# Angle tables grown on VectorE in 256 columns, set-up queues reordered, idle matmuls on zeros, one guard maximum and key copies shared out, in a kernel of multi-query attention beside a diagonal state-space layer

## The chip, the cores and the metric

The kernel runs on one core of a Trainium2 chip. The metric is device microseconds of one execution, lower is better. Engines: TensorE (PE, matmuls into PSUM), VectorE (DVE), ScalarE (ACT, activations), GpSimd (POOL) and SyncE (SP, which issues most DMAs; ScalarE's queue issues a few). Each engine takes its instructions in the order in which the program has them and waits on semaphores.

## What is computed

Two independent layers, whose outputs are put side by side (2048 x 1280, bf16). Layer A is a diagonal state-space layer: 640 complex states, a scan over 2048 steps, and a projection back. Layer B is attention with 32 heads of 20 columns that share one key and one value head:

```python
# A
Lam_bar = exp(dt * Lam)                       # 640 complex numbers
h[t] = Lam_bar * h[t-1] + x[t] @ B_bar.T      # 2048 steps
y = 2 * (h @ Cmat.T).real + x * Dskip
# B
q = (x @ wq).reshape(1, 2048, 32, 20)         # 32 heads
k, v = x @ wk, x @ wv                         # one head, 20 columns
o = softmax(q @ k.T * 20 ** -0.5) @ v
out = o.reshape(1, 2048, 640) @ wo
```

## The kernel before

Attention sets the course. Its scores are cut into 2048 units of 128 keys x 512 (query, head) columns: 32 groups (8 groups of 4 heads in each of 4 query blocks), each of 4 heads x 16 key blocks. A unit is filled by TensorE (QK) into a PSUM bank, turned into weights, and taken by TensorE into the PV accumulator. Most units go to ScalarE as an exponential (L1362) over a tile of three banks (R0) or two (R1), in turn; ten tiles of results (P) can be waiting for PV. The others go to VectorE, which makes the weights by integer arithmetic (L1368, then the shifts L1374). Such a unit is allowed only when the set-up work (`rest`) and the table growth (`grow`) are done. The first group is taken in two halves: group -1 has keys 0 to 1023 with a guard (a bound on the scores) from those keys alone, group 0 the other 1024 keys with the guard of all; a factor (`frac`, L649) joins them, and VectorE's L1411 carries the first half out of the accumulator.

The order on every engine is written by a planner in the program (`Plan`, `main`). It keeps a clock for each engine, prices each operation (`occ`) and takes from the candidates the one that could begin first, with a bias for each kind and some random noise; 64 seeds, one for each 64th of the units, set the biases and the noise. What it writes is fixed at build time: on the chip each engine follows that order and waits where a partner is late. The set-up up to the first exponential is written by hand in `setup`, in program order.

The set-up, by engine. SyncE issues ten transposing loads of B_x (`xbT`, blocks `0a` to `4a` of steps 0 to 1023, then `0b` to `4b`), then all of wq, then other things. ScalarE's queue issues log_dt, Lambda_im, wk, wv and the first 80 columns of wq. ScalarE pads wk to four heads (`wk4`, four copies, L521); the angle base table `tm` (128 steps, 5 blocks, sine and cosine) is made by VectorE (L753 to L756) and ScalarE (L758, L759). TensorE multiplies xbT by wk4 into B0 and B1 (512 keys each); VectorE takes the absolute maximum of each (L597) and makes the guard matrix Mblk from both (L605); ScalarE copies each twice to KT (L586); TensorE adds the guard to the queries of the first group in R0, VectorE copies them to QT (L846), and the first fill can start. `spin` matmuls (L553) between these write what nobody reads, into R0; they read wk4 and xbT.

Behind it, by the planner: the keys of the second half (`rest`: maximum over both banks L638, copies to KT by VectorE L590, the new guard `again`, 80 columns of wq, padded, as `wq1`, L651), the values (`vals`: 80 matmuls of 20 columns into PV, then four scaled copies to VP, L632), and the tables. The tables hold cos and sin for 512 steps: columns 0 to 127 are the base; each of the 30 other pieces of 128 columns is a product on GpSimd (L779, base times a rotation's sine) and a sum on VectorE (L781, base times its cosine plus or minus that product). Behind the 30 products GpSimd makes Md's mask (L690) and reorders wq to `wqd` (L656, five copies), from which later query groups are computed (`qd_block`).

## Time and profile before

| | |
|---|---|
| median of 3 runs | 762.35 us (760.70 to 762.83) |
| the profiled execution | 761.37 us |
| its span, first to last instruction | 759.5 us |
| mean granted TensorE clock | 0.988 |
| busy: TensorE, VectorE, ScalarE, GpSimd | 700.3, 716.0, 735.1, 369.4 us |
| ScalarE idle between the first and the last exponential | 11.4 us |
| first exponential starts, last one ends | 16.76, 750.82 us |

A timeline row gives the start in us, the time from the first to the last end of a run of like instructions, engine, line, operation, what it writes and reads with shapes, how many there are, and in brackets the idle time of the engine before it and who ended that. "PE R L453" as a releaser is a matmul into the score tiles. A row of windows gives a stretch, its length, the busy time of PE, weight loads, DVE, ACT and POOL with the number of instructions, the granted clock, the DMA share and GB/s.

### The profile page before, as it was taken

Reading aid. Unit: us, or ns where it says so; the run is one execution under the profiler, and the core shown is the slowest. Engines: PE = TensorE matmul, PEld = TensorE weight load, DVE = VectorE, ACT = ScalarE, POOL = GpSimd, SP = SyncE. Lnnn points to the kernel's source line nnn. Section 1 sums busy time; section 2 is a strip of 40 time slices with the busy share of each in tenths; the row PEclk is TensorE's granted clock in tenths of the full one; section 3 lists DMA queues with packets and bytes.
Section 4 is the critical chain, followed back from the end, with each engine's and each line's share of the span. In section 5 each row is a group of like instructions: output and inputs, shape, how many; then the busy total and the mean of one; then the engine's idle time right before and its main releaser. Section 6 shows DMA issues by size and latency. Waiting matters only on the chain.

```text
span 759.5 us, 22797 instructions
## 1 busy us (share of the span) xinstructions
PE 700.3 (92%) x9703; PEld 227.5 (30%) x9705; DVE 716.0 (94%) x1117; ACT 735.1 (97%) x702; POOL 369.4 (49%) x739
## 2 busy tenths in 40 slices
PE   6699997888899999999899999999999999989997
PEld 2222222222222334332222333332223333223433
DVE  5889999999998999999999899999999899999976
ACT  6769999999999999999999999999999999999996
POOL 7922235443998450009976602057982472880040
PEclk9979999999999999999999999999999999999999
DMA  9265601000002010230002011040000211000121
GB/s 178 61 109 120 129 22 45 13 23 3 16 10 66 17 43 29 57 60 15 16 10 51 25 35 40 18 93 23 3 16 22 76 33 33 18 15 9 37 54 36
DMA packets 61330, 31.89 MB, mean 42 GB/s; under 512 B 41638, under 2 KB 61230, under 8 KB 61230
## 3 DMA queue, kind: packets, MB, share of 16 engines
q1 hardware_dynamic: 59078, 30.12, 16.9%
q8 instruction: 77, 1.26, 0.7%
q10 hardware_dynamic: 2152, 0.32, 0.3%
q14 instruction: 23, 0.19, 0.1%
HBM read 9.21 MB, written 12.69 MB: 29 GB/s over the span
## 4 chain that ended last, share of the span: by engine, by line
ACT 78%; PE 12%; DVE 7%; POOL 2%; issue 1%; ACTq 0%
ACT P L1362 77%; PE B L453 5%; PE R L453 4%; PE PV L453 3%; DVE Pd L1374 2%; POOL Pd L779 2%; DVE Pd L1368 2%; DVE cs L781 1%; DVE tm L991 1%; DVE hh L1019 1%; ACTq L426 0%; DVE KT L590 0%; DVE VP L632 0%; ACT L515 0%; DVE mabs L638 0%
## 5 line engine op out<-in xcount | busy, mean ns | idle before, releaser
L1362 ACT ACTIVATE P<-R 128x1024 bf16<-128x1024 f32 (+1 forms) x677 | 722.3, 1297 | 11.4 <-PE R L453 7.2
L453 PE MATMUL R<-QT,KT 32*128 32x512 bf16 (+1 forms) x1684 | 266.2, 387 | 36.3 <-ACT P L1362 26.9
L453 PE MATMUL PV<-P,VP 128*32 128x512 bf16 x1586 | 270.7, 389 | 5.1 <-DVE VP L632 3.9
L453 PE MATMUL PV<-Pd,VP 128*32 128x512 bf16 x1848 | 269.4, 385 | 2.5 <-DVE OTr L1416 0.9
L1368 DVE TENSOR_SCALAR Pd<-B 128x512 int16<-128x512 f32 x364 | 246.1, 683 | 16.9 <-PE B L453 14.9
L1374 DVE TENSOR_SCALAR Pd<-Pd 128x1536 int16<-128x1536 int16 (+3 forms) x338 | 243.4, 727 | 2.8
L1007 POOL TENSOR_TENSOR tm<-hh,cs 128x128 bf16<-128x128 f32 x320 | 163.9, 535 | 156.9 <-DVE hh L1019 140.7
L453 PEld LDWEIGHTS R<-QT,KT 32*128 32x128 bf16 (+1 forms) x1684 | 66.4, 91 | 292.8 <-ACT P L1362 261.5
L453 PE MATMUL B<-QT,KT 32*128 32x512 bf16 x364 | 140.8, 387 | 0.0
L1007 POOL TENSOR_TENSOR W<-tm 128x128 bf16<-128x128 bf16 x160 | 81.6, 533 | 36.0 <-PE B L453 31.8
L453 PEld LDWEIGHTS PV<-Pd,VP 128*32 128x32 bf16 x1848 | 64.6, 94 | 66.4 <-issue 43.0
L453 PEld LDWEIGHTS PV<-P,VP 128*32 128x32 bf16 x1586 | 63.8, 94 | 57.9 <-issue 42.6
L1101 POOL TENSOR_TENSOR OTd<-OTd,rwide 128x128 bf16<-128x128 bf16 x80 | 33.6, 447 | 80.1 <-DMA OTd<-o_rows 78.2
L1368 DVE TENSOR_SCALAR Pd<-R 128x512 int16<-128x512 f32 x98 | 66.8, 682 | 2.3 <-PE R L453 2.0
L947 POOL TENSOR_SCALAR tm<-W,sc 128x128 f32<-128x128 bf16 x40 | 33.9, 860 | 55.8 <-DMA W<-in_A_C_im_dram 20.7
L991 DVE TENSOR_TENSOR tm<-B,cs 128x1024 bf16<-128x1024 f32 x40 | 48.5, 1214 | 0.8 <-PE B L453 0.7
L453 PE MATMUL B<-CGre,W 128*32 128x384 bf16 (+1 forms) x640 | 47.7, 303 | 0.1
L453 PE MATMUL B<-CGim,W 128*32 128x384 bf16 (+1 forms) x640 | 47.1, 299 | 0.0
L1019 DVE TENSOR_TENSOR_SCAN hh<-sc,hini,B 128x512 f32<-128x512 f32 x30 | 37.7, 1269 | 0.4 <-PE B L453 0.4
L453 PEld LDWEIGHTS B<-QT,KT 32*128 32x128 bf16 x364 | 33.0, 91 | 0.0
L453 PE MATMUL B<-xaT,BTim 128*32 128x512 bf16 x400 | 31.0, 383 | 0.0
L453 PE MATMUL B<-xbT,wqd 128*32 128x512 bf16 x400 | 30.8, 400 | 0.0
(163 smaller groups left out, 466.2 us busy)
## 6 DMA issues: line engine op xcount, KB each, us to landing
o_rows<-OTr SPq DMA_DIRECT2D x32, 128.0 KB, 1.7
QT<-q_rows SPq DMA_DIRECT2D x30, 128.0 KB, 2.3
q_rows<-Qd SPq DMA_DIRECT2D x16, 160.0 KB, 2.9
OTd<-o_rows SPq DMA_DIRECT2D x16, 160.0 KB, 3.3
out_dram<-ystage SPq DMA_DIRECT2D x16, 160.0 KB, 1.8
out_dram<-ostage SPq DMA_DIRECT2D x12, 160.0 KB, 1.8
CGre<-in_B_wq_dram SPq DMA_DIRECT2D x1, 800.0 KB, 7.2
WO<-in_B_wo_dram SPq DMA_DIRECT2D x4, 200.0 KB, 4.9
```

Source lines behind the costliest of these rows:

```text
L453: ins = e.matmul(o() if callable(o) else o, lhsT=l, rhs=r, start=st, stop=sp, skip_group_check=True, **kw)
L779: pool(lambda e, c=c, i=i, s=s, tmp=tmp: e.tensor_scalar(tmp, K.base[:, 1 - i, c, :], s, None, op0=ALU.mult), self.base_keys + ["rot"], [t ...
L781: grow.append(Op("dve", lambda e, c=c, i=i, co=co, tmp=tmp, k=k: e.scalar_tensor_tensor(out=K.cs[:, c, i, 128 * k:128 * k + 128], in0=K.ba ...
L947: pool(lambda e, y=y, c=c, gy=gy, i=i: e.tensor_scalar(K.ctmp[:, i:i + 128], y[:, i:i + 128], sc[:, gy, c:c + 1], None, op0=ALU.mult), key ...
L991: dve(lambda e, k=k, h=h: e.tensor_tensor(K.tm[:, 2 * k:2 * k + 2, :], bass.AP(tensor=K.BB, offset=512 * int(h.key[1]), ap=[[512 * self.BA ...
L1007: put(lambda e, c0=c0, end=end: e.tensor_tensor(out[:, c0:end], a[:, c0:end], b[:, c0:end], op), reads, [writes + h], n, gate=None if i el ...
L1019: dve(lambda e, ri=ri, ini=ini, h=h: e.tensor_tensor_scan(K.hh[:, ri, :], dec, h.T[:, :], ini, ALU.mult, ALU.add), ["sc", None, "hini"], [ ...
L1101: ops.append(Op("pool", lambda e, c=c, m=m: e.tensor_tensor(K.OTd[:, m, c], K.OTd[:, m, c], K.rwide[:, c], ALU.mult), rw + [f"OTe{dd}" for ...
L1362: return Op("act", lambda e: e.activation(dst, K.R[n % 2][:, 0:512 * size], ACT.Exp, scale=self.exp_scale), [f"R{n % 2}"] + ["R0c"] * (siz ...
L1368: return Op("dve", lambda e: e.tensor_scalar(K.Pd[:, 0, u, :], K.B[x][:, :], self.d_off, 0.0, op0=ALU.add, op1=ALU.max), [key], [f"Pd{u}_0 ...
L1374: return Op("dve", lambda e: e.tensor_scalar(K.Pd[:, i:i + n, a:b, :].rearrange("p s u n -> p s (u n)"), K.Pd[:, 0:n, a:b, :].rearrange("p ...
```

## The change

1. Growth of the tables: no product on GpSimd. VectorE makes 15 products of 256 columns (sine and cosine together, fp32) and 15 sums of 256 columns; a third base plane holds the negated first one (one more VectorE operation), so that both halves are a subtraction.
2. Queues: wv's load goes from ScalarE's queue to SyncE's, between the two halves of xbT. On GpSimd half_pi comes first, and the zeros in OTr's second half come right behind the identity.
3. wk4 is filled by one VectorE copy instead of four ScalarE copies.
4. Idle matmuls read the identity and those zeros, and there are 14 instead of 9: three at the very start, three after the bias rows, one among the key matmuls; the four and three behind stay.
5. One maximum over both banks (1024 columns) instead of two and a combination; the guard product is a tensor_scalar.
6. Keys 512 to 1023 are copied to KT by VectorE, behind the query copy, instead of by ScalarE. KT is tracked in blocks of 128 keys; group 0 may start when the new queries are there and a fill waits only for its own keys.
7. The planner's biases for `rest`, `vals` and `grow` differ, and all but a few of the 64 seeds. So the order of everything behind the set-up is another one. The whole order has 447 two-bank exponentials instead of 445, with 232 three-bank ones as before.

VectorE, from the end of its memsets to the first VP copies and the new query copy, before:

```order
L597 TENSOR_REDUCE mabs<-B 128x1 x2
L605 SCALAR_TENSOR_TENSOR Mblk<-mabs,Pd 128x128
L846 TENSOR_SCALAR QT<-R 128x512
L763 CAST cs<-tm 128x10x128
L781 SCALAR_TENSOR_TENSOR cs<-tm,rot,Pd 128x128 x19
L632 TENSOR_SCALAR VP<-PV 128x16x20 x4
L617 TENSOR_TENSOR mabs<-mabs 128x1
L638 TENSOR_REDUCE mabs<-B 128x1
L617 TENSOR_TENSOR mabs<-mabs 128x1 x2
L590 TENSOR_SCALAR KT<-B,half 128x512 x2
```

The same stretch now (the line numbers are those of the changed file; L789 is a product, L791 a sum):

```order
L859 TENSOR_SCALAR QT<-R 128x512
L588 TENSOR_SCALAR KT<-B,half 128x512 x2
L615 TENSOR_SCALAR tm<-tm 128x640
L772 CAST cs<-tm 128x10x128
L789 TENSOR_SCALAR Pd<-tm,rot 128x256 x2
L791 SCALAR_TENSOR_TENSOR cs<-tm,rot,Pd 128x2x128
L789 TENSOR_SCALAR Pd<-tm,rot 128x256
L791 SCALAR_TENSOR_TENSOR cs<-tm,rot,Pd 128x2x128
L789 TENSOR_SCALAR Pd<-tm,rot 128x256
L791 SCALAR_TENSOR_TENSOR cs<-tm,rot,Pd 128x2x128
L643 TENSOR_REDUCE mabs<-B 128x1
L618 TENSOR_TENSOR mabs<-mabs 128x1 x2
```

Nineteen sums stood ahead of VP; now four products and three sums stand ahead of the second maximum, and behind it come two key copies, the guard product and VP.

GpSimd, behind the constants of the mask, before:

```order
L576 TENSOR_TENSOR sc<-sc,sv 128x5
L779 TENSOR_SCALAR Pd<-tm,rot 128x128 x30
L688 MEMSET Md 128x160
L690 AFFINE_SELECT Md<-Md 128x160 x4
L656 COPY wqd<-CGre 128x640 x5
```

And now:

```order
L603 TENSOR_TENSOR sc<-sc,sv 128x5
L693 MEMSET Md 128x160
L695 AFFINE_SELECT Md<-Md 128x160 x4
L661 COPY wqd<-CGre 128x640 x5
L664 TENSOR_SCALAR nident<-ident 128x128
```

The five copies to wqd stand right behind Md's mask; they wait for the load of wq.

VectorE, ahead of the copy to wq1 (L651 before, L656 now), before:

```order
L646 TENSOR_SCALAR Mblk<-Pd,mabs 128x128
L781 SCALAR_TENSOR_TENSOR cs<-tm,rot,Pd 128x128 x3
L651 COPY wq<-CGre 128x20x20
L781 SCALAR_TENSOR_TENSOR cs<-tm,rot,Pd 128x128 x4
L842 TENSOR_SCALAR Qabs<-B 128x512
```

And the last rows ahead of it now:

```order
L789 TENSOR_SCALAR Pd<-tm,rot 128x256
L820 RECIPROCAL sc<-sc 128x5
L791 SCALAR_TENSOR_TENSOR cs<-tm,rot,Pd 128x2x128
L789 TENSOR_SCALAR Pd<-tm,rot 128x256
L791 SCALAR_TENSOR_TENSOR cs<-tm,rot,Pd 128x2x128
L656 COPY wq<-CGre 128x20x20
```

Between the mask product (L651 now) and that copy stand eight sums, seven products and the reciprocal, where three sums stood; behind it three products and four sums, the last ones around the query copies.

The core of the diff:

```diff
-    SPIN = 1, 4, 3
+    SPIN = 3, 3, 1, 4, 3
+    HEAD = 8
-    SEEDS = (111, 1209, 2445, 3180, 4815, 5028, 6775, 7124, 8575, 9354, 10399, 11278, 12878, 13810, 14176,
+    SEEDS = (172, 1183, 2925, 3286, 4369, 5158, 6349, 7538, 8807, 9403, 10689, 11086, 12883, 13390, 14424,
...
         for i, h in enumerate("ab"):
+            if i:
+                go(self.dma(K.wv_raw, t["wv"].rearrange("(c p) n -> p c n", p=128), "wv", writes=["wv_raw"], kb=25))
             for c in range(NC):
...
-        go(self.dma(K.wv_raw, t["wv"].rearrange("(c p) n -> p c n", p=128), "wv", writes=["wv_raw"], kb=25, q="act"))
...
+        def spin(n):
+
+            for i in range(n):
+                go(self.mms([self.m1(K.R[0][:, 0:512], K.ident[:, :], K.OTr[:, 1, :], True, True)], ["ident", "OTr1"], ["R0"],
+                            accum=True))
...
-        for j in range(4):
-            act(lambda e, j=j: e.activation(K.wk4[:, :, 32 * j:32 * j + 20], K.wk_raw[:, :, :], ACT.Copy),
-                ["wk_raw", "wk4"], ["wk4"], n=100)
...
-        for i in range(2):
-            dve(lambda e, i=i: e.tensor_reduce(out=mcol(i), in_=K.B[i][:, :], axis=AX.X, op=ALU.max,
-                                               apply_absolute_value=True), [f"B{i}"], [f"mabs{i}"], n=512)
+        dve(lambda e: e.tensor_reduce(out=mcol(3), in_=K.BB[:, 0:h0], axis=AX.X, op=ALU.max, apply_absolute_value=True),
+            ["B0", "B1"], ["mabs3"], n=h0)
...
-        for tb in range(2):
-            for o in copy("act", tb):
-                go(o)
...
+        for o in copy("act", 0):
+            go(o)
...
+        dve(lambda e: e.tensor_scalar(K.Mblk[:], K.mask, mcol(3), None, op0=ALU.mult), mk + ["mabs3"], ["Mblk"], n=128)
...
+        for o in copy("dve", 1):
+            go(o)
+        dve(lambda e: e.tensor_scalar(K.base[:, 2], K.base[:, 0], -1.0, None, op0=ALU.mult), self.base_keys, self.base_keys, 640, 2)
...
+        dve(lambda e: e.tensor_copy(wk4[:, :, :, 0:20], wk), ["wk_raw", "wk4"], ["wk4"], n=400)
...
-                for i in range(2):
-                    m = 2 * (3 * c + k - 1) + i
-                    tmp, tk = K.flat[:, 4608 + 128 * m:4736 + 128 * m], f"gt{m}"
...
-                    pool(lambda e, c=c, i=i, s=s, tmp=tmp: e.tensor_scalar(tmp, K.base[:, 1 - i, c, :], s, None, op0=ALU.mult),
-                         self.base_keys + ["rot"], [tk], 0.385)
...
+                prods.append(Op("dve", lambda e, c=c, s=s, tmp=tmp: e.tensor_scalar(tmp, K.base[:, 1:3, c, :], s, None, op0=ALU.mult),
+                                self.base_keys + ["rot"] + rows, [tk], occ=dve_t(256, 1.4)))
+                sums.append(Op("dve", lambda e, c=c, co=co, tmp=tmp, k=k: e.scalar_tensor_tensor(
+                    out=K.cs[:, c, :, 128 * k:128 * k + 128], in0=K.base[:, 0:2, c, :], scalar=co, in1=tmp, op0=ALU.mult,
+                    op1=ALU.subtract), self.base_keys + ["rot", tk] + rows, [f"cs{c}{i}{k}" for i in range(2)],
+                    occ=dve_t(256) + 0.06))
...
-                reads |= {f"KT{j % 2}_{kc // 4}", f"QT{g % self.QRING}"}
+                reads |= {f"KT{j % 2}_{kc}", f"QT{g % self.QRING}"}
...
-                    bias = 0.0 if own else self.wait - 0.1 * (name == self.first)
+                    bias = (0.12 if name == "vals" else -0.4 * (o is again[0]) if name == "rest" else 0.0) if own else self.wait - 0.1 * (name == self.first)
...
+                elif name == "grow":
+                    bias = 0.3 if rest or self.vals else 0.05
```

More of the change, by code (lines that the diff above doesn't have):

```diff
@@ L417, in do, with dma @@
         self.go(Op(*a, **k))
[L419 removed]
+    def dma(self, out_ap, in_ap, key, reads=(), writes=(), tr=False, kb=100, q="sp", lat=None, **k):
         nc = self.nc
@@ L601, in setup @@
               occ=act_t(512), lat=0.12))
-        for tb in range(2):
-            for o in copy("act", tb):
-                go(o)
-        dve(lambda e: e.scalar_tensor_tensor(out=K.Mblk[:], in0=wide(1), scalar=mcol(0), in1=K.mask, op0=ALU.max,
-                                             op1=ALU.mult), mk + ["mabs0", "mabs1"], ["Mblk"], n=128)
-        spin(self.SPIN[1])
+        for o in copy("act", 0):
+            go(o)
+        s, lre, NRE = self.s_ops[0], self.s_ops[3], 1
+        pool(lambda e: e.tensor_tensor(s(NRE), s(0), lre, ALU.mult), ["sc", "sv0"], ["sc"])
+        act(lambda e: e.activation(s(self.RDEC), s(NRE), ACT.Exp), ["sc"], ["sc"], n=5)
+        dve(lambda e: e.tensor_scalar(K.Mblk[:], K.mask, mcol(3), None, op0=ALU.mult), mk + ["mabs3"], ["Mblk"], n=128)
+        spin(self.SPIN[3])
         va = [self.v_part(0, c) for c in range(NC)]
@@ L620, in setup @@
         top.done = lambda: self.max_done.add(0)
-        last = list(copy("dve", 3))
-        last[-1].done = lambda: self.qt_done.add(0)
+        more, last = (list(copy("dve", i)) for i in (2, 3))
+        self.kt_ready = self.HEAD
+        for x, n in ((more, 12), (last, 16)):
+            x[-1].done = lambda n=n: setattr(self, "kt_ready", n)
         self.max_done = set()
@@ L1444, in main @@
                     out, d = pick(size, d)
+                if g in qt_done and all(left[gx][j][-1] < self.kt_ready for gx, j in out):
                     o = fill_op(n, out, d, x)
```

129 lines of the change are left out of this document (66 added, 63 removed), and 8 rows, old and new, of the table SEEDS.

## The prediction

> **What bounds the kernel now.** I read the page first (its shares, the chain that ended last, the costliest groups), then ScalarE's busy time stage by stage, then each engine's timeline of the first 50 us.
>
> ```profile
> span 759.5 us, 22797 instructions
> ...
> ACT 78%; PE 12%; DVE 7%; POOL 2%; issue 1%; ACTq 0%
> ...
> L1362 ACT ACTIVATE P<-R 128x1024 bf16<-128x1024 f32 (+1 forms) x677 | 722.3, 1297 | 11.4 <-PE R L453 7.2
> ...
> L453 PE MATMUL PV<-P,VP 128*32 128x512 bf16 x1586 | 270.7, 389 | 5.1 <-DVE VP L632 3.9
> ```
>
> The exponentials on ScalarE hold 722.3 of 759.5 us and are 78% of the chain. In the next table (stretch, its length, then each engine's busy time) the ACT column shows where they are not fed.
>
> ```profile
> 16.80:25.00 8.20, 6.54 (x90) 3.23 (x89) 6.68 (x19) 8.19 (x7) 7.83 (x13) 1.00 0.54 173
> 25.00:50.00 25.00, 18.45 (x159) 4.48 (x160) 22.69 (x40) 14.77 (x14) 16.80 (x29) 0.73 0.46 67
> 50.00:250.00 200.00, 179.97 (x2177) 51.40 (x2178) 193.52 (x296) 199.60 (x184) 104.28 (x186) 0.99 0.21 46
> 250.00:500.00 250.00, 241.62 (x3566) 80.80 (x3563) 242.47 (x373) 249.56 (x240) 100.28 (x210) 1.00 0.13 33
> 500.00:750.80 250.80, 238.72 (x3511) 79.63 (x3503) 238.80 (x363) 250.51 (x236) 127.59 (x267) 1.00 0.12 31
> 750.80:759.50 8.70, 5.49 (x174) 4.14 (x170) 3.35 (x6) 1.43 (x3) 0.00 (x0) 0.94 0.22 77
> ```
>
> From 50 to 750.8 us ScalarE idles 0.40 + 0.44 + 0.29 = 1.1 us. From 25 to 50 it idles 10.2 us. The span is therefore a sum: start of the first exponential, 722.3 us of exponentials, 10.2 + 1.1 us of waits, 0.4 us of another activation, and 8.7 us of tail. The change can reach the first and third terms. ScalarE's timeline:
>
> ```profile
> 14.34 2.41 ACT L586 ACTIVATE KT<-B,half 128x512 bf16<-128x512 f32 x4
> 16.76 8.23 ACT L1362 ACTIVATE P<-R 128x1536 bf16<-128x1536 f32 x7
> 28.18 1.02 ACT L1362 ACTIVATE P<-R 128x1024 bf16<-128x1024 f32 x1 [3.19 <-PE R L453]
> 39.85 2.36 ACT L1362 ACTIVATE P<-R 128x1536 bf16<-128x1536 f32 x2 [2.42 <-PE B L453]
> 44.95 1.02 ACT L1362 ACTIVATE P<-R 128x1024 bf16<-128x1024 f32 x1 [2.73 <-PE R L453]
> ```
>
> TensorE, in whose order these waits arise:
>
> ```profile
> 7.90 1.04 PE L453 MATMUL B<-xbT,WO 128*128 128x512 bf16 x2 [2.63 <-ACT WO L521]
> 13.31 1.03 PE L453 MATMUL R<-xbT,WO 128*128 128x512 bf16 x4
> 15.11 0.39 PE L453 MATMUL R<-Qabs,Mblk 128*128 128x512 bf16 x1 [0.58 <-ACT KT L586]
> 27.42 0.40 PE L453 MATMUL PV<-P,VP 128*32 128x512 bf16 x4 [3.92 <-DVE VP L632]
> 37.59 1.67 PE L453 MATMUL B<-xbT,wq 128*32 128x512 bf16 x20 [2.13 <-DVE wq L651]
> 42.29 0.62 PE L453 MATMUL B<-Qabs,Mblk 128*32 128x512 bf16 x4 [1.40 <-DVE Qabs L842]
> ```
>
> VectorE, which is waited for there:
>
> ```profile
> 5.72 0.85 DVE L753 TENSOR_TENSOR Pd<-hh,ang 128x640 f32<-128x640 f32 x1
> 6.60 0.49 DVE L754 TENSOR_SCALAR Pd<-Pd 128x640 f32<-128x640 f32 x1
> 13.08 1.29 DVE L597 TENSOR_REDUCE mabs<-B 128x1 f32<-128x512 f32 x2 [2.56 <-PE B L453]
> 14.48 0.48 DVE L605 SCALAR_TENSOR_TENSOR Mblk<-mabs,Pd 128x128 bf16<-128x128 f32 x1
> 17.53 4.69 DVE L781 SCALAR_TENSOR_TENSOR cs<-tm,rot,Pd 128x128 bf16<-128x128 f32 x14
> 22.73 1.51 DVE L781 SCALAR_TENSOR_TENSOR cs<-tm,rot,Pd 128x128 bf16<-128x128 f32 x3 [0.50 <-POOL Pd L779]
> 25.69 1.67 DVE L632 TENSOR_SCALAR VP<-PV 128x320 bf16<-128x320 f32 x4
> 27.41 1.21 DVE L638 TENSOR_REDUCE mabs<-B 128x1 f32<-128x1024 f32 x1
> 28.93 1.40 DVE L590 TENSOR_SCALAR KT<-B,half 128x512 bf16<-128x512 f32 x2
> 30.25 0.28 DVE L643 TENSOR_SCALAR Mblk<-Pd,mabs 128x128 bf16<-128x128 f32 x1
> 34.10 3.06 DVE L781 SCALAR_TENSOR_TENSOR cs<-tm,rot,Pd 128x128 bf16<-128x128 f32 x3
> 37.36 4.27 DVE L781 SCALAR_TENSOR_TENSOR cs<-tm,rot,Pd 128x128 bf16<-128x128 f32 x4
> ```
>
> GpSimd, on whose products the first sums wait and beside whose copies the last ones run:
>
> ```profile
> 12.55 19.69 POOL L779 TENSOR_SCALAR Pd<-tm,rot 128x128 f32<-128x128 f32 x30
> 34.34 6.76 POOL L656 COPY wqd<-CGre 128x640 bf16<-128x640 bf16 x5
> ```
>
> VectorE is held at GpSimd's pace in the middle of the 19 table sums that stand ahead of VP, so VP comes late, TensorE stands 3.92 us at its first PV matmul, and the fills behind it starve ScalarE (3.19 us). Later the sums that run beside GpSimd's five wqd copies delay wq1 and Qabs, and TensorE stands there (2.13, 1.40).
>
> **The change, part by part.** *Start.* The wv issue (0.78, below) leaves ScalarE's queue and half_pi becomes GpSimd's first constant, so the first table load, and with it the angle chain, comes about 0.8 us earlier: L753's work at 4.9 instead of 5.72. The padded key weights follow as one VectorE copy and are ready near 6.0, where ScalarE's four copies released TensorE at 7.9. Then the data decides; issues on SyncE's and ScalarE's queues, and the median time to landing:
>
> ```profile
> 0.79 13.78 SPq L424 DMA_TRANSPOSE xbT<-in_B_x_dram  x10
> 2.11 0.78 ACTq L426 DMA_DIRECT2D WO<-in_B_wv_dram  x1
> ```
>
> ```profile
> xbT<-in_B_x_dram SPq DMA_TRANSPOSE x10, 4.1
> ...
> CGre<-in_B_wq_dram SPq DMA_DIRECT2D x1, 800.0 KB, 7.2
> WO<-in_B_wv_dram ACTq DMA_DIRECT2D x1, 25.0 KB, 4.6
> ```
>
> The fifth transpose is issued at 0.79 + 4 x 1.38 = 6.3 and lands at 10.4. Behind it stand two matmuls. Warm, four take 1.03 us (the row at 13.31); cold, two take 1.04 (7.90). With idle matmuls from about 2 us on I take warm: the first 1024 keys are complete at 11.0 instead of 13.08, where the maximum began. From there the old chain (maximum, mask product, guard matmul, query copy, first fill) took 16.76 - 13.08 = 3.7 us. It loses 0.1 (one maximum, 1.21 for 1.29) and 0.2 (the mask product as L643 has it, 0.28 for 0.48): 3.4. wv is now issued behind five transposes at 7.7 and lands near 12.4; its first eight matmuls stand ahead of the guard matmul in TensorE's queue and let it through at 12.8, 0.2 after the mask product is ready (11.0 + 1.21 + 0.28 and 0.1 between); every fill is queued behind them. ScalarE has two key copies instead of four (1.2 us less): from the maximum's end at 12.2 on, 2.41/2 and some 0.4 more, ready at 13.8; 0.6 of cover hides the added VectorE copy in the angle chain. The keys 512 to 1023, now copied by VectorE behind the query copy, are there at 15.2, and the seventh tile is the first to read them, past 20. First exponential at 14.4: **-2.4** (bounds -0.5, all still cold, and -3.0).
>
> *Waits up to 28 us.* VectorE then does two key copies (1.40), the negation (0.49), the cast, four products and three sums before it takes the second maximum. A product of 256 columns: 640 take 0.49, so 0.2 to 0.3; a sum of 256: 0.34 for 128 (4.69/14, GpSimd's products beside it) plus up to 128 x 0.85/640 = 0.17 by L753, so 0.40 to 0.50. With the cast priced at L753's rate (1280 columns, at most 1.7) that is 15.2 + 0.5 + 1.7 + 4 x 0.25 + 3 x 0.45 = 19.7. The second five transposes, 0.6 later behind wv, land by 0.79 + 0.6 + 9 x 1.38 + 4.1 = 17.9, so the second maximum does not wait for them; 1.8 us of cover. Maximum, key copies, mask product, VP: 1.21 + 0.4 + 1.40 + 0.28, first VP at 23.0. Ten P buffers hold the first ten tiles; seven tiles (18 banks) took 8.23 us, so ten (25 banks) end near 14.4 + 11.3 = 25.7, and the eleventh needs VP at 25. The 3.19 and the two small waits (0.50, 0.25) go.
>
> *Table growth against the wqd copies.* What is late next is wq1. The wq load is issued 0.6 later (wv ahead of it), lands at 15.2 + 7.2 = 22.4, and GpSimd, without the 30 products, copies wqd from 22.4 to 29.2 instead of 34.34 to 41.1. Beside these copies a sum took (3.06 + 4.27)/7 = 1.05 on average against 0.34: about one VectorE table operation passes per copy. In the new order a product, two mask products and a sum meet them; VectorE reaches the remaining run near 29.8. From there to the wq1 copy stand seven sums, seven products and a reciprocal, 7 x 0.45 + 7 x 0.25 + 0.2 = 5.1: wq1 at 34.9, its twenty matmuls (1.67) end at 36.5, the fill behind them at 36.9. That is the eighteenth tile; ScalarE has finished the seventeenth (43 banks at 0.455, and the 0.6 of the other activation) at 34.4. Wait: 2.5 (bounds 0 and 4). Behind it the same queue order as before costs a wait for Qabs and one for the wqd block, 0.6 and 0.7, and 0.4 for small ones. Sum 4.2 instead of 10.2: **-6.0** (bounds -10 and -2). The Trainium skill, "SBUF — State Buffer", section Who interferes with whom, says that a VectorE operation with two SBUF inputs, or in a two-port mode, and a GpSimd operation that reads SBUF take one port pair in turn, each blocking the other for its whole length. By that rule the fp32 products are blocked as well, which no row here shows, and it is the rule that speaks against the move: without it the wait of 2.5 would be 0. The trace agrees for the sums (1.05 against 0.34).
>
> *TensorE's clock.* 25 to 50 us ran at a granted clock of 0.73, beside the long stands; with shorter stands the 20 wq1 matmuls may take 1.1 instead of 1.67. I leave that 0.6 out. The Trainium skill, "TensorE: Matmul & The Clock Gate", section What's actually happening, has half clock after an idle window of 3.4 us and full clock after a busy one; by it the idle matmuls warm the array before the keys arrive, and the sum would take 0.6 more off.
>
> *Exponentials.* The new order has 447 two-bank exponentials for 445: four units, 4 x 722.3/1586 = **+1.8**. VectorE gives up four units, its table work and two key copies roughly fill that. *Nothing:* R1 matmul order, wq1's zeroing, the finer keys of KT: all hidden behind the waits above. Tail: same operations, 0 (bounds -0.5, +0.5). The main part has new random seeds and so another order; I take 0 (bounds -1, +5).
>
> Sum: -2.4 - 6.0 + 1.8 = -6.6. The profiled execution took 761.37 and would take 754.8. The median shown is 762.35, 0.98 above it; the same step gives **755.7**.
>
> **The rivals.** *The port turn does not bite* (products unblocked, or wq lands late enough): the 2.5 and the two waits behind it vanish, 4 more off, 751.5, down to 749.5 if the clock holds too. For it: VP and the key copies read PSUM and were not slowed. Against: the seven sums. 0.12.
>
> *The start does not move*: zeros do not warm TensorE, or wv lands late (each us beyond 12.4 is a us on the first exponential), and only the waits go: 755.7 + 2 = 757.7, to 759.5 with a wait of 4 at wq1. For: cold, the 17 matmuls would take until 12 us. 0.13.
>
> *The new order of the main part loses it*: TensorE works in fixed order, and 700 us are ordered anew. Before, they lost 1.1 us. TensorE is busy 239 to 242 of 250 there, so a block set ahead of a fill delays ScalarE by its own length, 0.2 to 0.4. It decides at some 20 such places (6.6 us); at 30 the kernel is slower: 765. For: the order was drawn for set-up times that the port turn breaks. Against: the same planner lost only 1.1 before, after a far worse set-up, and ScalarE kept 99.8%. 0.20, of which 0.08 slower than before by over 0.3% (2.3 us, about what a measurement of this kernel can tell from no change) and 0.12 within that.
>
> **How the numbers follow.** Forecast 0.55, rivals 0.12, 0.13, 0.20. The first three are faster: 0.80; the fourth gives 0.12 and 0.08. The range takes in the forecast with its bounds on wq1 (2.5 fewer or 1.5 more) and start (up to 1.9 more), the second rival, half of the first and the near part of the third: 751 to 761.
>
> **What would show it.** Right: key maximum done near 12.2, first exponential near 14.4, no GpSimd release among VectorE's idle in the tables, PV's first stand gone, one stand of 2 to 3 us at wq1 near 36, wqd copies at 22 to 29 with a stretched table operation beside each, ScalarE idle under 5 us between 25 and 50 and about 1 after. Wrong: idle of ScalarE over 4 us after 50; a first exponential past 16; table operations at their bare length beside the copies.

## The result, and the profile after

The changed kernel takes 754.87 us (median of 4 runs, 753.83 to 755.11), the kernel before 762.22 (4 runs): ratio 0.9904, 95% interval 0.9887 to 0.9921, 7.3 us less. The profiled execution took 755.11 (761.37 before). The forecast was 755.7, and 754.8 for the profiled execution. The total was hit, in part by luck: three of its terms were off, and their errors nearly cancel.

The page of the changed kernel, its first line, its chain of waits by engine, and the group of the exponentials:

```profile
span 753.3 us, 22628 instructions
...
ACT 78%; DVE 13%; PE 7%; POOL 1%; issue 1%; DMA 0%; SPq 0%; POOLq 0%; DVEq 0%
...
L1375 ACT ACTIVATE P<-R 128x1024 bf16<-128x1024 f32 (+1 forms) x679 | 724.2, 1296 | 5.4 <-PE R L454 4.0
```

Stretches of the changed kernel, from its first exponential to the end of the last and the tail (columns as in the table before):

```profile
15.13:25.00 9.87, 8.66 (x98) 3.60 (x98) 9.77 (x21) 9.87 (x9) 2.68 (x3) 0.91 0.70 188
25.00:50.00 25.00, 24.10 (x268) 6.46 (x268) 24.73 (x53) 23.54 (x23) 12.31 (x28) 0.83 0.58 78
50.00:744.30 694.30, 649.28 (x9055) 207.47 (x9047) 668.20 (x1019) 691.14 (x651) 324.46 (x643) 1.00 0.14 36
744.30:753.30 9.00, 5.18 (x168) 3.67 (x164) 3.27 (x6) 1.41 (x2) 0.00 (x0) 1.00 0.22 76
```

The same sum as before the change can be read off. Start 15.13 (16.76): -1.6. ScalarE idle from 25 to 50, 25 - 23.54 = 1.46 (10.2): -8.8. Exponentials 724.2 (722.3): +1.9. Idle after 50, 694.30 - 691.14 = 3.2 (1.1): +2.0. Tail 9.0 (8.7): +0.3. Together -6.2, as the span fell. This is one execution against one; how far executions of one order differ is read from the experiments.

ScalarE's timeline, changed kernel:

```profile
15.13 13.90 ACT L1375 ACTIVATE P<-R 128x1536 bf16<-128x1536 f32 x12 [0.80 <-PE R L454]
29.26 3.71 ACT L1375 ACTIVATE P<-R 128x1536 bf16<-128x1536 f32 x3 [0.24 <-PE R L454]
...
36.03 1.02 ACT L1375 ACTIVATE P<-R 128x1024 bf16<-128x1024 f32 x1 [0.31 <-PE R L454]
37.70 14.57 ACT L1375 ACTIVATE P<-R 128x1536 bf16<-128x1536 f32 x13 [0.64 <-PE R L454]
62.46 16.77 ACT L1375 ACTIVATE P<-R 128x1536 bf16<-128x1536 f32 x16 [0.65 <-PE R L454]
79.46 221.18 ACT L1375 ACTIVATE P<-R 128x1536 bf16<-128x1536 f32 x204 [0.24 <-PE B L454]
```

The waits of 3.19, 2.42 and 2.73 are gone; 0.31 and 0.64 stand where wq1 and the new queries are made. A new wait of 0.65 stands at 62.46. TensorE, from the key matmuls to the first guard, and at wq1:

```profile
8.69 1.05 PE L454 MATMUL B<-xbT,WO 128*128 128x512 bf16 x2
9.77 0.82 PE L454 MATMUL R<-xbT,ystage 128*128 128x512 bf16 x3
11.08 0.59 PE L454 MATMUL B<-xbT,WO 128*128 128x512 bf16 x2
13.47 0.39 PE L454 MATMUL R<-Qabs,Mblk 128*128 128x512 bf16 x1 [0.54 <-DVE Mblk L605]
34.41 1.26 PE L454 MATMUL B<-xbT,wq 128*32 128x512 bf16 x20 [0.33 <-DVE wq L656]
```

Two key matmuls take 1.05 at 8.69 and 0.59 at 11.08: TensorE becomes fast only at about 9.7 (slow here means a matmul of 512 columns each 0.43 us, fast one each 0.22). The guard matmul waits for Mblk, not behind wv's matmuls. VectorE and GpSimd, changed kernel:

```profile
11.71 1.23 DVE L595 TENSOR_REDUCE mabs<-B 128x1 f32<-128x1024 f32 x1 [1.67 <-PE B L454]
...
22.82 0.90 DVE L648 TENSOR_SCALAR Mblk<-Pd,mabs 128x128 bf16<-128x128 f32 x1
23.64 1.67 DVE L635 TENSOR_SCALAR VP<-PV 128x320 bf16<-128x320 f32 x4
25.23 1.09 DVE L789 TENSOR_SCALAR Pd<-tm,rot 128x256 f32<-128x256 f32 x1
...
29.33 0.34 DVE L789 TENSOR_SCALAR Pd<-tm,rot 128x256 f32<-128x256 f32 x1
29.59 0.47 DVE L791 SCALAR_TENSOR_TENSOR cs<-tm,rot,Pd 128x256 bf16<-128x256 f32 x1
...
34.00 0.35 DVE L656 COPY wq<-CGre 128x400 bf16<-128x400 bf16 x1
```

```profile
22.32 6.54 POOL L661 COPY wqd<-CGre 128x640 bf16<-128x640 bf16 x5 [9.45 <-DMA CGre<-in_B_wq_dram]
```

Beside GpSimd's copies a mask product takes 0.90 and a table product 1.09, where alone they take 0.28 and 0.34; the VP copies between them, which read PSUM, keep their 1.67.

### The profile page after: what moved, and what is told of

Same layout as the page of the kernel before. It is cut to its first block, busy times and chain, and to the rows that moved or that the text cites. A ratio compares the mean times of both kernels' runs of the same rounds, so it can differ in the third digit from the quotient of the medians.

```text
span 753.3 us, 22628 instructions
## 1 busy us (share of the span) xinstructions
PE 699.1 (93%) x9628; PEld 225.5 (30%) x9630; DVE 714.4 (95%) x1121; ACT 734.8 (98%) x698; POOL 349.4 (46%) x709
## 3 DMA queue, kind: packets, MB, share of 16 engines
q8 instruction: 77, 1.26, 0.7%
## 4 chain that ended last, share of the span: by engine, by line
ACT 78%; DVE 13%; PE 7%; POOL 1%; issue 1%; DMA 0%; SPq 0%; POOLq 0%; DVEq 0%
ACT P L1375 77%; DVE Pd L1381 3%; DVE Pd L1387 3%; PE R L454 3%; PE B L454 2%; PE PV L454 2%; DVE hh L1032 1%; DVE cs L791 1%; DVE tm L1004 1%; DVE Qd L876 1%; POOL tm L1020 1%; DVE Pd L789 1%; DVE KT L588 1%; POOL W L1020 0%; DMA q_rows<-Qd 0%
## 5 line engine op out<-in xcount | busy, mean ns | idle before, releaser
L1375 ACT ACTIVATE P<-R 128x1024 bf16<-128x1024 f32 (+1 forms) x679 | 724.2, 1296 | 5.4 <-PE R L454 4.0
L454 PE MATMUL PV<-Pd,VP 128*32 128x512 bf16 x1832 | 263.5, 385 | 2.1 <-DVE OTr L1429 1.0
L454 PE MATMUL PV<-P,VP 128*32 128x512 bf16 x1590 | 262.8, 391 | 0.3
L454 PEld LDWEIGHTS PV<-P,VP 128*32 128x32 bf16 x1590 | 62.1, 94 | 54.2 <-issue 44.8
L1381 DVE TENSOR_SCALAR Pd<-R 128x512 int16<-128x512 f32 x92 | 62.6, 681 | 2.0 <-PE R L454 1.6
L454 PE MATMUL B<-xaT,BTre 128*32 128x512 bf16 x400 | 31.3, 383 | 1.3 <-DVE Pd L1381 0.5
```

The costliest lines, as they stand in the source:

```text
L454: ins = e.matmul(o() if callable(o) else o, lhsT=l, rhs=r, start=st, stop=sp, skip_group_check=True, **kw)
L1375: return Op("act", lambda e: e.activation(dst, K.R[n % 2][:, 0:512 * size], ACT.Exp, scale=self.exp_scale), [f"R{n % 2}"] + ["R0c"] * (siz ...
L1381: return Op("dve", lambda e: e.tensor_scalar(K.Pd[:, 0, u, :], K.B[x][:, :], self.d_off, 0.0, op0=ALU.add, op1=ALU.max), [key], [f"Pd{u}_0 ...
```

## The experiments

Twelve kernels. In eight of them the planner's order stands, but for the instructions that are named below as added, shortened or moved, so that they can be laid beside the changed kernel place by place; in the other four (products on GpSimd twice, growth alone, old seeds) everything behind the set-up is ordered anew. Each was timed beside the kernel before. The three columns of us are of one profiled execution each, read from ScalarE's timeline and stretches; the ratio is of all runs:

| run | first exponential | ScalarE idle 25 to 50 | idle after 50 | ratio to before, 95% |
|---|---|---|---|---|
| kernel before | 16.76 | 10.2 | 1.1 | 1 |
| changed kernel | 15.13 | 1.5 | 3.2 | 0.9887 to 0.9921 |
| e1 no idle matmuls | 16.14 | 2.1 | 2.6 | 0.9906 to 0.9934 |
| e2 two more idle matmuls | 15.34 | 1.5 | 3.1 | 0.9905 to 0.9932 |
| e3 idle matmuls on ones | 15.49 | 2.6 | 2.3 | 0.9902 to 0.9931 |
| e10 dense idle matmuls | 14.25 | 4.4 | 2.5 | 0.9901 to 0.9940 |
| e12 the same, stores first | 14.74 | 1.2 | 4.3 | 0.9905 to 0.9932 |
| e11 stores first | 15.47 | 2.5 | 3.2 | 0.9944 to 0.9971 |
| e5 short GpSimd copies | 14.43 | 0.3 | 9.5 | 0.9936 to 0.9967 |
| e6 more GpSimd copies | 14.74 | 7.3 | 2.1 | 0.9955 to 0.9977 |
| e4 products on GpSimd | 14.58 | 6.3 | 14.2 | 1.0266 to 1.0294 |
| e4b the same, early | 15.23 | 5.3 | 5.5 | 1.0159 to 1.0188 |
| e8 growth alone | 17.66 | 6.9 | 9.1 | 1.0271 to 1.0308 |
| e9 old seeds | 15.02 | 3.1 | 7.4 | 1.0191 to 1.0229 |

### Do idle matmuls on zeros warm TensorE?

e1 cuts the first seven idle matmuls to 10x10, in their places:

```diff
-            go(self.mms([self.m1(K.R[0][:, 0:512], K.ident[:, :], K.OTr[:, 1, :], True, True)], ...
+                o.fn = (lambda e: e.matmul(K.R[0][0:10, 0:10], lhsT=K.ident[0:10, 0:10], rhs=K.OTr[0:10, 1, 0:10], ...
```

> The changed kernel with its first seven idle matmuls on zeros cut to 10x10, nothing else moved on any engine. Theory A (they warm TensorE, which came after some 4.4 us of dense work from 5.30 on, at 9.7): dense work now begins at 6.55, key matmuls stay at a pitch of 0.43 us until 10.9, the key maximum starts at 12.1 instead of 11.71, first exponential near 15.5, total +0.4. Theory B (zeros count for nothing; the clock rises 3.1 us after the first key matmul, 7.90 to 11.0 in the kernel before and 6.55 to 9.7 in the changed one): nothing moves, maximum at 11.7, first exponential 15.1, total within 0.2.

TensorE's timeline in e1:

```profile
9.26 1.46 PE L454 MATMUL R<-xbT,ystage 128*128 128x512 bf16 x3
10.51 1.06 PE L454 MATMUL B<-xbT,WO 128*128 128x512 bf16 x2
11.79 0.90 PE L454 MATMUL B<-xbT,WO 128*128 128x512 bf16 x2
```

The key matmuls are slow to about 12.2; the maximum starts at 12.72 (11.71), the first exponential at 16.14. Theory A holds and is even undersized (first exponential +1.0 for +0.4): idle matmuls on zeros count, since 12.2 lies outside the 8.2 to 10.2 of the seven executions below that have them in full. The total hardly moved (0.9920 for 0.9904, the intervals overlap), a first sign that the start is not what the end hangs on.

e2 puts two more between the 10x10 matmul and the bias rows:

```diff
-        go(ones(0))
-        go(ones(1))
+        for o in [self.mms([self.m1(K.R[0][:, 0:512], K.ident[:, :], K.OTr[:, 1, :], True, True)], ...) for _ in "12"]: ...
+        go(ones(0)); go(ones(1))
```

> The changed kernel with two more idle matmuls on zeros between the 10x10 matmul at 3.84 and the bias rows, so that TensorE has work from 2.08 to the keys almost without a gap; all other orders are the same. Theory A: dense work from 3.84 or earlier, fast from about 8.2 on, keys complete near 10.8 instead of 11.7, first exponential near 14.2, total -0.9. Theory B: the key matmuls begin up to 0.5 us later behind the two, the clock rises 3.1 us after them, maximum at 11.9, first exponential 15.1 to 15.5, total 0 to +0.4.

Fast from 9.3, but the keys began 0.6 later (7.18), first exponential 15.34. That lies in Theory B's 15.1 to 15.5 and misses Theory A's 14.2, but B's clock would have risen 3.1 us after 7.18, at 10.3: it tells neither theory from the other. e3 lets the same seven read ones:

```diff
-            ... K.ident[:, :], K.OTr[:, 1, :], True, True ...
+            ... K.ident[:, :], K.P[:, 0, :], True, True ...     # K.P[:, 0, :] filled with 1.0
```

> The changed kernel with its first seven idle matmuls reading ones instead of zeros (a small VectorE fill more, so that they start near 2.4); all other orders are the same. Theory B with data (only matmuls whose data switch count): fast 3.1 us after 5.30 at the latest, that is at 8.4, keys complete near 10.8, first exponential near 14.3, total -0.8. Theory A, or B for all idle matmuls: the same as on zeros, fast at 9.7, first exponential 15.1 to 15.2.

Fast from 10.0, having started 0.8 later: the data made no gain that one execution can show. Of e3's theories the one in which data count (14.3) missed, but by less than executions differ. Runs e4, e4b, e5, e6, e9 and e11 have the changed kernel's order of matmuls up to there, and TensorE became fast in them between 8.2 and 10.2, with first exponentials from 14.43 to 15.47. Three of these (e5, e6, e9) ran on one chip and still differ by 1.4 us (8.2 to 9.6). So the moment is a draw of each execution, spread over some 2 us, and the forecast's 14.4 was its early edge. e10 makes TensorE busy from 2.08 to the keys, with the one-row bias matmuls moved behind the fourth key matmul:

```diff
+        idle(1)
         self.constants(dve, act, pool)
...
-        go(ones(0))
-        go(ones(1))
+        go(ones(0, False))
+        go(ones(1, False)); bias_rows = self.p.ops["pe"][-2:]; del self.p.ops["pe"][-2:]; idle(2)
...
             if c == 1:
-                spin(self.SPIN[2])
+                self.p.ops["pe"].extend(bias_rows); spin(self.SPIN[2])
```

> The changed kernel with idle matmuls on zeros from 2.08 to the first key matmul almost without a gap (one more ahead of the 10x10 matmul, two more behind it) and the two bias rows moved from there to behind the fourth key matmul; all other orders are the same. Theory W (the clock rises when a window of some 3 us was full of matmuls, the window's phase differs between executions of one order: 9.6 in the changed kernel, 8.2 in the run with the products on GpSimd, which has the same first 30 matmuls; the one-row bias matmuls do not count): fast before 8.9 in every execution, keys complete by 10.8 (the fifth block lands at 10.1), first exponential near 14.1, total -0.4 to -1.0. Theory X (only the key matmuls themselves count): fast 3.1 us after the first of them, at 9.6 or later, first exponential 15.1 to 15.4, total within 0.3.

TensorE's timeline in e10, and in e12, which has the same start:

```profile
6.26 1.18 PE L454 MATMUL B<-xbT,WO 128*128 128x512 bf16 x4
10.09 0.61 PE L454 MATMUL B<-xbT,WO 128*128 128x512 bf16 x2
```

```profile
6.26 1.27 PE L454 MATMUL B<-xbT,WO 128*128 128x512 bf16 x4 [0.15 <-DVE WO L768]
...
10.61 0.61 PE L454 MATMUL B<-xbT,WO 128*128 128x512 bf16 x2 [0.29 <-DMA xbT<-in_B_x_dram]
...
65.66 0.39 PE L454 MATMUL R<-QT,KT 32*128 32x512 bf16 x2 [2.22 <-DMA QT<-q_rows]
```

Theory W holds for the start: fast during the first four key matmuls in both, and in e12 the last keys wait for the landing of xbT. The first exponential came at 14.25 and 14.74. The gain in time did not come: 0.9921 and 0.9918. The Trainium skill, "TensorE: Matmul & The Clock Gate", section What's actually happening, says that the clock rises after a busy window of about 3.4 us that runs on its own, whatever the kernel does; the runs agree in the draw, and show 2 us of spread where the section speaks of 0.5 to either side and, for one kernel, of 6, 11 or 14 slow matmuls.

### What do the GpSimd copies cost?

e5 cuts the wqd copies to a tenth (the rest of wqd stays zero), e6 puts a second copy ahead of each:

```diff
-  e.tensor_copy(K.wqd[:, c, :].rearrange("p (d h) -> p d h", h=32), K.wq_raw[:, c, :].rearrange("p (h d) -> p d h", d=20))
+e5 e.tensor_copy(K.wqd ...[:, 0:2, :], K.wq_raw ...[:, 0:2, :])
+e6 [e.tensor_copy(x[:, c, 0:32 * n] ..., K.wq_raw ...[:, 0:n, :]) for x, n in ((K.Qd, 16), (K.wqd, 20))]
```

> The changed kernel with a second GpSimd copy (128x512, to a tile not yet in use) ahead of each wqd copy, so that the copies last from 22.3 to about 34 instead of 28.9; no order moves. Theory P: through 29 to 34 about one VectorE SBUF operation passes per copy, four or five instead of twelve, so wq1's copy comes near 37 instead of 34.0 and ScalarE waits 2.5 to 3.5 us there instead of 0.31; total +2 to +3.5. If the products are not blocked (only the sums): half of that, +1 to +1.5. Theory without a port turn: wq1's copy at 34.0, total within 0.3.

VectorE's timeline in e6, and ScalarE's:

```profile
28.24 1.55 DVE L791 SCALAR_TENSOR_TENSOR cs<-tm,rot,Pd 128x256 bf16<-128x256 f32 x1
29.72 1.19 DVE L789 TENSOR_SCALAR Pd<-tm,rot 128x256 f32<-128x256 f32 x1
30.83 1.57 DVE L791 SCALAR_TENSOR_TENSOR cs<-tm,rot,Pd 128x256 bf16<-128x256 f32 x1
32.33 1.20 DVE L789 TENSOR_SCALAR Pd<-tm,rot 128x256 f32<-128x256 f32 x1
...
38.48 0.35 DVE L656 COPY wq<-CGre 128x400 bf16<-128x400 bf16 x1
```

```profile
41.79 1.02 ACT L1375 ACTIVATE P<-R 128x1024 bf16<-128x1024 f32 x1 [6.37 <-PE R L454]
```

One table operation passes per copy, product and sum alike: 1.19 and 1.55 for 0.34 and 0.47. wq1 comes 4.5 us later, ScalarE waits 6.37, and the total is 0.9966 for 0.9904, +4.7 us. Theory P holds, with more than its price: wq1's copy came 1.5 later than priced, and the twenty wq1 matmuls ran slow here (2.32 for 1.26). "SBUF — State Buffer" of the Trainium skill, section Who interferes with whom, has this turn; the run agrees, for fp32 products too.

> The changed kernel with GpSimd's five wqd copies cut to a tenth of their columns (the rest of wqd is left at zero, so later groups' queries are wrong); no order moves. Theory P (the copies stretch VectorE's SBUF operations: 0.90, 1.09, 0.78 and 0.54 us where they take about 0.28, 0.35, 0.28 and 0.47 alone): 1.9 us less, wq1's copy at 32.1 instead of 34.0, the waits of 0.31 and 0.64 behind it shrink, total -0.3 to -0.9 against the changed kernel. Theory Q (ScalarE is by then late enough that nothing of this reaches it): the same operations short, but the total within 0.3. The first 40 matmuls are those of the changed kernel, so this is also another draw of its start.

The operations ran at their bare length (0.28, 0.34, 0.27, 0.47), wq1's copy came at 31.35, and ScalarE idled 0.3 us from 25 to 50: P's mechanism. Both totals were wrong: e5 is slower than the changed kernel, 0.9952 for 0.9904. ScalarE and SyncE in e5, then SyncE in the changed kernel (DMA issues; the second column is the time taken by the issues):

```profile
65.07 2.54 ACT L1375 ACTIVATE P<-R 128x1536 bf16<-128x1536 f32 x2 [5.42 <-PE R L454]
68.96 2.37 ACT L1375 ACTIVATE P<-R 128x1536 bf16<-128x1536 f32 x2 [1.35 <-PE B L454]
```

```profile
25.34 0.42 SPq L427 DMA_DIRECT2D m_row<-mabs  x1
...
29.92 1.76 SPq L427 DMA_DIRECT2D md<-m_row  x4
...
57.95 2.44 SPq L427 DMA_DIRECT2D q_rows<-Qd  x4
```

```profile
24.76 0.42 SPq L427 DMA_DIRECT2D m_row<-mabs  x1
...
26.42 2.01 SPq L427 DMA_DIRECT2D md<-m_row  x4
28.48 12.58 SPq L425 DMA_TRANSPOSE xaT<-in_A_x_dram  x7
...
55.14 3.02 SPq L427 DMA_DIRECT2D q_rows<-Qd  x4
...
60.77 0.58 SPq L427 DMA_DIRECT2D q_rows<-Gs  x1
62.60 0.82 SPq L427 DMA_DIRECT2D QT<-q_rows  x2
```

From 25 us on SyncE issues transposes back to back, most of them 1.3 us each, and the first computed query rows go out and come back in between. That queue hardly cares when ScalarE began: with first exponentials from 14.25 (e10) to 16.14 (e1) the stores leave at 54.37 and 54.54, and in the changed kernel at 55.14. (It does wait where an engine is late, in e6 3.7 us for VectorE.) In the changed kernel VectorE's next Qd copy waits for them, TensorE's fill waits for VectorE, and ScalarE's 0.65 at 62.46 follows:

```profile
60.59 0.69 DVE L876 TENSOR_SCALAR Qd<-B 128x512 bf16<-128x512 f32 x1 [1.30 <-DMA q_rows<-Qd]
...
62.02 0.39 PE L454 MATMUL R<-QT,KT 32*128 32x512 bf16 x3 [0.98 <-DVE Pd L1381]
```

In e5 the md loads leave 4.6 us behind m_row's store instead of 1.7, because SyncE stands 2.9 us until m_row has landed. The queue is 1.5 us later at its first BTre transpose (42.63 for 41.10) and, with one transpose of 2.56 us where it took 1.13, 2.8 us later at the stores. ScalarE, 2.2 us earlier, waits 5.42. That profile is of the slowest of e5's six executions (756.20 to 759.49 us). In e1, e3 and e10 ScalarE came late enough not to wait at this place.

### Is SyncE's queue the floor?

e11 moves the four stores ahead of the three transposes before them, e12 does so on e10. As the order of SyncE's queue:

```diff
-DMA_TRANSPOSE BTim, BTre, BTim; q_rows<-Qd x4; DMA_TRANSPOSE BTre, BTim; q_rows<-Gs; QT<-q_rows x2
+q_rows<-Qd x4; DMA_TRANSPOSE BTim, BTre, BTim; DMA_TRANSPOSE BTre, BTim; q_rows<-Gs; QT<-q_rows x2
```

> The changed kernel with the four stores of the first dense query block (q_rows<-Qd) moved on SyncE's queue ahead of the three BT transposes before them; nothing else moves. Theory F (these transposes run back to back from 28 to 61 us whatever ScalarE does; the stores wait behind them until 55.1, VectorE's next Qd copy waits for the stores, and ScalarE's 0.65 at 62.46 is that): stores at 52.2, no wait of ScalarE between 55 and 64, the exponential that stood at 79.5 to 80.2 in all runs with this order at 78.8 to 79.3, total -0.4 to -0.8 against the changed kernel. Theory G (the later wait has another cause, or the transposes put behind are missed at once): the 0.65 stays or returns before 80 us, total within 0.3.

> The same move of the four stores, on the kernel with the dense idle matmuls and the bias rows behind the fourth key matmul. Theory F: first exponential near 14.2 again, and the gain of the start is kept past 62 us unless wq1 eats it; total -0.5 to -1.6 against the changed kernel. Theory H (the start is given back at wq1 between 34 and 41, where the twenty matmuls run at half speed when the clock is down, 2.3 us instead of 1.26): ScalarE idle 3 to 4.5 us from 34 to 42 again, total within 0.5 of the changed kernel.

The 0.65 went, as F said. The totals did not follow it: e11 (0.9957) is slower than the changed kernel, where F and G both missed, and e12 (0.9918) misses F's gain and can't be told from the changed kernel. The stores now hold SyncE until Qd is there, all five transposes stand behind them, and q_rows<-Gs leaves at 63.07 and 61.73 instead of 60.77. TensorE then waits 1.60 (e11) and 2.22 (e12, above at 65.66) for QT. In e12 ScalarE stood 1.6 us ahead of the changed kernel at the exponential that begins at 62.46 there, and 1.75 behind it at the one of 79.46. So F's cause was right and its edit wrong: in these two runs the queue's whole content up to QT is the floor, not the place of the stores. e11's profile (755.82) is of the fastest of its five executions, so what its slower ones (to 759.01) lost besides was not seen. Letting some BT transposes go behind the QT loads was not tried. H's loss at wq1 showed in e10 (4.4 us idle from 25 to 50) and in e11, not in e12; in e11:

```profile
34.67 2.32 PE L454 MATMUL B<-xbT,wq 128*32 128x512 bf16 x20 [1.42 <-DVE wq L656]
```

The same twenty matmuls took 1.26 in the changed kernel, e5 and e12. The clock in the 4 us before them, in the changed kernel and in e10 (TensorE's busy time stands behind the length, the granted clock third from the end):

```profile
30.41:34.41 4.00, 3.67 (x29) 0.59 (x26) 4.00 (x14) 4.00 (x6) 1.90 (x7) 0.62 0.05 0
```

```profile
30.16:34.16 4.00, 1.42 (x18) 0.32 (x15) 4.00 (x14) 4.00 (x5) 2.08 (x8) 0.87 0.05 0
```

In the changed kernel TensorE went through 26 to 33 us at a granted clock of 0.50, hence busy throughout, and had just become fast. In e10 it was fast in that stretch (0.98), so it had little to do (4.72 of 7 us busy), stood, and had fallen to 0.50 when wq1 came. So an early gain of TensorE can be given back at wq1. The busy time alone does not decide it: with 2.70 us of those 4 e12 stayed fast, with 2.79 e4b did not, and why is open. ScalarE waited 2.02 there in e11, 2.77 in e10, 0.31 in the changed kernel.

### Which part removed the waits?

e4 and e4b keep the change but put the products back on GpSimd (e4 left them waiting behind the negated plane until 15.9; e4b lets them start at 10.7). e8 is the kernel before with only the growth moved.

```diff
-                prods.append(Op("dve", ... e.tensor_scalar(tmp, K.base[:, 1:3, c, :], s, None, op0=ALU.mult) ...
+                    self.do("pool", ... e.tensor_scalar(tmp, K.base[:, 1 - i, c, :], s, None, op0=ALU.mult) ...
```

> The changed kernel with the table products back on GpSimd (30 of 128 columns, and 30 sums of 128 on VectorE), the rest of the change kept; the planner orders everything behind the set-up anew, so start, waits and later idle are read apart. First exponential unchanged at 15.1 in both theories. Theory C (the gain in the waits came from the order, VP and the keys ahead of most sums): with seven sums instead of four products and three sums ahead of the second maximum VP starts by 23.5, the stand at the first PV does not come back, ScalarE idles 1.5 to 4 us from 25 to 50. Theory D (it came from taking the products from GpSimd): VectorE is again held at 0.66 us a sum, VP later than 25, ScalarE idles 7 us or more from 25 to 50. Later than 50 us its idle is 1 to 5 either way, with other random draws of the order; total 754 to 759 by C, 760 to 765 by D.

> The changed kernel with the table products on GpSimd as in the earlier run, but without the negated base plane, behind which they had waited until 15.9: they start near 10.8. The planner orders the rest anew (twelve sums now ahead of the second maximum, seven ahead of wq1), so only the first 50 us are compared. Theory C (the order of VP and keys against the sums made the gain): VP starts by 24.5, no stand of over 1 us at the first PV, products done near 30.5, wqd copies 33 to 40, wq1's copy near 32; ScalarE idles 1 to 3.5 us from 25 to 50. Theory D (products off GpSimd made it): sums held at 0.63 to 0.66 us, VP at 25 or later, ScalarE idles over 5 us from 25 to 50. The total tells nothing of this; with an order not drawn for it I expect 765 to 790.

> The kernel before with only the growth of the tables changed (15 products and 15 sums of 256 columns on VectorE, one negation), old set-up, old biases, old seeds; the planner orders the rest anew, and puts VP behind four sums and the second maximum behind eleven. Only the first 50 us are compared. First exponential at 16.2 to 17.5 as before. If the growth by itself makes the gain in the waits (D): VP near 23, the stand of 3.92 at the first PV gone, ScalarE idle from 25 to 50 falls from 10.2 to 4 or less. If the order of keys and VP is needed as well (C): the second maximum comes near 27 and the keys 1024 to 2047 after 28, TensorE stands at the first matmul on the new queries, ScalarE idles 5 us or more. Total 760 to 785 by the draw of the order.

Stretch from 25 to 50 us in e4b, and in e8:

```profile
25.00:50.00 25.00, 21.19 (x250) 6.47 (x253) 23.47 (x49) 19.73 (x18) 20.97 (x43) 0.89 0.53 80
```

```profile
25.00:50.00 25.00, 20.01 (x200) 5.18 (x198) 22.24 (x46) 18.14 (x18) 11.61 (x28) 0.82 0.46 62
```

ScalarE idles 5.3 (e4b) and 6.9 (e8), where it idled 10.2 before and 1.5 after. In e4 and e4b VP starts at 23.98 and 23.94 and the 3.92 at the first PV stays away, as C said; but TensorE is slow at the twenty wq1 matmuls in both (2.33), and the queries come late: in e4b behind ten sums that run beside the wqd copies (Qabs at 35.33), in e4 because wq1's copy comes only at 35.91. The waits are 1.96 and 2.45 in e4b and 4.61 in e4. In e8 VP is early too (21.46), and the second maximum comes at 32.50, so the new keys and guard are late (one wait of 5.62). Neither theory alone: the growth by itself takes off 3.4 us, the rest of the change without it 5.0, and both together 8.8. The shares are rough: each is one execution of an order drawn anew, and the old seeds alone (e9, below) idle 3.1 where the changed kernel idles 1.5. e8's start, 17.66, lies outside what was expected, with the same matmuls up to there as in the kernel before (16.76): TensorE became fast near 13 us instead of 11. e4's total (782.71) missed both theories; e4b's (774.88) and e8's (783.45) lay in the wide ranges given for them, far up for a reason that the last run shows.

e9 puts the 64 old seeds into the changed kernel:

```diff
-    SEEDS = (172, 1183, 2925, 3286, ...
+    SEEDS = (111, 1209, 2445, 3180, ...
```

> The changed kernel with the 64 seeds of the kernel before, nothing else; the planner orders everything behind the set-up anew. Theory S (the order behind the set-up is a draw, and the new seeds are what keeps ScalarE fed in it): start as before at 14.5 to 15.6, but ScalarE's idle after 50 us rises from 3.2 to between 6 and 20, or more of the units fall to ScalarE, total 760 to 785. Theory T (any seeds do about as well): idle after 50 within 1 to 5 us, total 753 to 757.

The group of the exponentials in e9:

```profile
L1375 ACT ACTIVATE P<-R 128x1024 bf16<-128x1024 f32 (+1 forms) x685 | 740.5, 1322 | 11.3 <-PE R L454 4.4 <-PE B L454 3.1 <-PE PV L454 3.1
```

777.60 us, 1.021 of before: theory S. ScalarE's busy time rises by 16.3 us, because VectorE takes 421 units instead of 458 (37 x 0.455 = 16.8); ScalarE's idle rises by 1.6 between 25 and 50 and by 4.2 after it. e4, e4b and e8, with orders not drawn for them either, have 433, 433 and 428 such units and 735 to 736 us of exponentials.

## Why the prediction was right, and where not

The profiled execution was to fall by 6.6 and fell by 6.3. That this came so near is luck: the errors are +0.8 (start), -2.8 (waits), +0.1 (exponentials), +2.0 (main part) and +0.3 (tail), and those that have stated bounds lie inside them. The terms are also not independent, as the forecast took them. In the changed kernel and e1, e2, e3, e10, e11 and e12 the start and both idle columns of the table add to 19.8 to 21.2 us (28.1 before), though the starts differ by 1.9: what is gained early is given back at wq1 or at SyncE's queue. Of the signs named beforehand, tables without a wait for GpSimd, PV's first stand gone, copies at 22 to 29 with stretched operations beside them and idle under 5 us came; a maximum done by 12.2 (it was 12.94), a stand of 2 to 3 us at wq1 and about 1 us of idle after 50 did not.

*Start, forecast -2.4, measured -1.6.* The step that failed is the warm TensorE ("with idle matmuls from about 2 us on I take warm"). The fifth block, issued at 6.51, landed 3.6 us later, at 10.1 (10.4 in the forecast), but TensorE was slow until 9.7 and finished the keys at 11.7 instead of 11.0. From the maximum to the first exponential it took 3.42, the forecast's 3.4. wv did not bind; its matmuls were done before the guard's. The forecast treated a draw as a fixed time: seven executions with these first matmuls gave 14.43 to 15.47, with a mean of 14.9, and the keys' maximum began at 11.01 in e5. The old start is a draw too (16.76, and 17.66 in e8), and against the mean of those two the seven are 2.3 earlier. e1 puts some 1 us of it to the idle matmuls; the other parts of the new set-up were not taken out one by one.

*Waits, forecast -6.0, measured -8.8.* The mechanism was right: VP at 23.64 (23.0), no stand at the first PV, copies at 22.3 to 28.9, a product, two mask products and a sum stretched beside them, wq1's copy at 34.00 (34.9). The mis-sized term is the stand at wq1, 2.5 forecast and 0.31 measured: VectorE came 0.9 earlier, ScalarE 0.7 later from its start, and the twenty matmuls took 1.26 instead of 1.67. With the clock down the same order waited 2.02 (e11) and 2.77 (e10), so the forecast's 2.5 was within what that place does. All idle from 25 to 50 was 1.2 to 4.4 in the changed kernel, e1 to e3 and e10 to e12, so -8.8 is one draw between -9.0 and -5.8; of the kernel before there is only the one profile.

*Exponentials, forecast +1.8, measured +1.9.* The four units, as counted.

*Main part, forecast 0, measured +2.0.* Of this 0.65 is SyncE's queue at 62.46, which the forecast did not look at: it walked the queues of four engines and took DMAs only by their landing. The rest stands at places that return in the runs of this order, 0.24 to 0.5 each; that they belong to the order is what their return suggests, and it was not tested further. *Tail:* +0.3 for 0.

*The rivals.* The port turn bites, in products as in sums (e6); in the changed kernel ScalarE's later start hid most of it, so its absence would not have given the 4 us which that rival priced: e5 took the turn away, stood 2.2 us ahead at 60 us, 0.7 of it from its start, and lost that and more at SyncE's queue. "The start does not move" came half true for the time: between 14.25 and 16.14 the first exponential made no difference that the totals show (0.9904 to 0.9921). The third rival, a new order that loses the main part, did not come for the seeds chosen, but its price and mechanism were wrong. I counted stalls of 0.2 to 0.4; with the old seeds e9 shows a loss of 23 us, most of it because VectorE is given fewer units. That the chosen seeds avoided this could not be read from the profile of before; a count of the units per engine in the new order (458 for 462) could be, and was the better evidence against that rival.

## What to carry to other kernels

When a stage is shortened, list every queue that runs at its own pace beside it, the DMA issuer's too, and ask at which time each next needs the stage: the gain ends at the first one. A time that hangs on TensorE's clock is a draw and wants a range. When an order written by a planner is drawn anew, count how many units each engine gets before counting stalls.

## What the runs showed of the hardware

The moment at which TensorE becomes fast differed by some 2 us between executions of one order of matmuls (8.2 to 10.2), and the same twenty matmuls took 1.26 where TensorE had been busy 3.67 of the 4 us before them (the changed kernel) and 2.32 where it had been busy 1.42 (e10). Idle matmuls on zeros brought it forward: 12.2 in the one execution without them, 8.2 to 10.2 with them, and before 7.5 with an almost gapless row of them from 2.08 on (e10, e12). A fp32 tensor_scalar from SBUF to SBUF is held by a GpSimd copy about as long as a two-input operation is (0.34 to 1.19, and up to 1.41 in e8, beside 0.47 to 1.55). The loads that wait for one small store, m_row, left 1.7 us behind it in the changed kernel and 4.6 in e5; why it landed so late there was not found, and whether e5's other executions had it too is not known.
